# Induced attention and an ELU feed-forward: the opening stage rebuilt

## The chip, the core and the metric

The kernel runs on one core of one Trainium2 chip. The metric is the device time of one execution in microseconds; the kernel before has a median of 1762.04 us over 3 runs (1761.57 to 1762.32). Five engines have queues of their own: PE multiplies matrices, ACT evaluates functions, DVE and POOL work element by element, and SP issues the DMAs. An engine takes its instructions strictly in the order in which they stand in its queue.

## The reference

The input x has 4 batches of 12480 rows of 128 channels, in float32. A set of 32 learned rows ("inducing") first attends to all rows of a batch; then all rows attend to the 32 results. The output goes through a feed-forward layer of 2048 hidden units with an ELU between its two weights. Both weights arrive as float64.

```python
def mab(q, kv):
    s = scale * (q @ kv.transpose(0, 2, 1))
    s = s - s.max(-1, keepdims=True)
    a = np.exp(s); a /= a.sum(-1, keepdims=True) + 1e-09
    return a @ kv
h = mab(I, x)                  # 32 rows per batch
y = mab(x, h)                  # 12480 rows per batch
h1 = y @ w_in                  # 128 -> 2048
g = np.where(h1 > 0, h1, np.exp(np.minimum(h1, 0)) - 1)
return g @ w_out               # 2048 -> 128
```

## The kernel before, in words

A batch is cut into 25 blocks of 512 or 480 rows, gathered into 7 groups of up to 4 blocks (`GROUPS`). For every block the feed-forward runs over 8 units; a unit is a pair of 128-wide chunks of the 2048 hidden units. Within a unit, PE makes two chunks of the hidden layer in PSUM (line 560), ACT takes the exponential (568), DVE joins it with the hidden value (574), ACT rounds the result to a high part (583), DVE or POOL makes the low part (586, or 591 and 596), and PE multiplies both with the second weight, itself split into a high and a low part (618). After 8 units DVE transposes the block's output out of PSUM (625) and SP stores it. PE runs up to 5 units ahead with line 560. The feed-forward's output for the first unit is issued once three further units have gone into PE (`RAMP`).

While the feed-forward of one batch runs, the first attention of the next batch is worked on beside it, in steps that are placed by hand at fixed units (`first_half`, `attend`): x pieces come through two buffers (`xqp`, tag "xq"), DVE transposes them (241), PE makes scores (293), and so on. The first batch has nothing to hide behind. Its first attention stands alone in front of everything, in `first_batch`, together with the conversion of both weights from float64. This opening stage is what the change touches.

The opening, in program order, is this. SP loads half of the first weight, then x in 14 pieces (two into the buffers "xm", the others into buffers that the feed-forward uses later), then the other half. For each of the 7 groups PE transposes the pieces, ACT and DVE copy them out (270), PE makes the scores (293), ACT copies them (302), and DVE takes their maximum (306). The softmax over all 12480 rows is done in two phases (`PHASES`): groups 0 to 2 use the maximum of these three groups, groups 3 to 6 use the maximum over all, and the first phase's sum is then rescaled. `bias_of` makes the two maxima into biases (318, 324, 326). For each group ACT takes the exponential (347), DVE transposes it (360), and PE gathers the weighted sum of the rows (369), which DVE adds up (378, 380, 385). The sum is normed (411) and spread (417), giving hT4. The second attention for block 0 alone (`lone`) goes through lines 485, 493, 501, 502, 505, 512 to 515, 523, 526 and 528 and ends in the first "stack", the moving operand of line 560. `project_h` multiplies hT4 with the converted first weight (427), and `stack_h` copies the product by 12 DMAs (449) into `hw`, the stationary operand of line 560.

The weights are read as pairs of 32-bit words and converted with integer and float instructions, in slices of 256 columns (`WS`), eight slices for each weight. For each slice `take_apart` uses DVE for exponent (158) and mantissa bits (168), ACT for the sign (162), the low word (163) and two clamps of the exponent (164, 165), and POOL for the scale (172). `put_together` multiplies sign and scale on POOL (180), joins the words on DVE (181) and multiplies both on POOL (185). For the second weight ACT copies each 128-column chunk as the high part (212, 215), and POOL subtracts for the low part (216). All slices pass through two buffers ("w_part", in the pool `op`). Slices of the first weight are called for after each group's scores, one for each group. The second weight is loaded in four quarters, two into "xm" buffers and two into buffers of group 1's x pieces, all of which come free only once the gathers have read them; it is converted before the lone attention in program order.

The order in which instructions enter the queues of ACT, DVE, POOL and SP is not the program order. A planner simulates the kernel ahead of time: when an engine is free in that simulation, it takes the ready instruction that stands first in the program. On the chip this order is then fixed, whatever is ready. From the first feed-forward unit on PE's order is that of the program.

## Time and profile before

| | |
|---|---|
| median of 3 runs | 1762.04 us |
| profiled execution: time | 1761.6 us |
| profiled execution: span of all its instructions | 1759.5 us |
| PE busy in the span | 1659.5 us (94%) |
| DVE busy | 1551.8 us (88%) |
| ACT busy | 1425.0 us (81%) |
| POOL busy | 1331.7 us (76%) |

The span runs from the first to the last instruction that the profiler recorded; 2.1 us of the execution lie outside it. Busy time is what an engine's instructions took, without the issuing of DMAs. A busy PE is not necessarily at its peak, since its matmuls are pipelined. In rows of the trace, `out<-in` names the tiles that an instruction writes and reads, L12 is line 12 of the kernel before, and `[1.35 <-POOL ...]` says that the engine had stood idle for 1.35 us until that instruction of POOL released it.

### The profile page before, as it was taken

The page shows a single profiled execution, that of the slowest core. Times are in us where ns is not written, and L with a number is a line of the kernel's source. Part 1 is how long each engine was busy: PE and PEld are TensorE (multiplying, and loading weights), DVE is VectorE, ACT ScalarE, POOL GpSimd, SP SyncE. Part 2 cuts the span into 40 slices and gives each one's busy share as a digit, 9 for nine tenths or more (in the row PEclk, how much of TensorE's full clock was granted, in tenths as well). Part 3 has the DMA queues.
Part 4 walks back from the last instruction along what each step waited for, and adds up shares of the span by engine and source line. Part 5 has one row for each costly group of instructions (what it writes and reads, how often), then busy time and mean ns, then how long its engine had stood idle before and what let it go on. Part 6 is the DMA issues. An engine that isn't in the chain of part 4 may idle for free.

```text
span 1759.5 us, 22797 instructions
## 1 busy us (share of the span) xinstructions
PE 1659.5 (94%) x7480; PEld 1177.4 (67%) x7480; DVE 1551.8 (88%) x1635; ACT 1425.0 (81%) x1662; POOL 1331.7 (76%) x955
## 2 busy tenths in 40 slices
PE   6699999999999999999999999999999999989897
PEld 4356666677766766767676666667777776667676
DVE  6899989888999898889899998988899988888886
ACT  6778888788887887878787888878888888888786
POOL 3978877777787777777787787777778887766665
PEclk9599999999999999999999999999999999999999
DMA  7362323323234224232225232321221211111111
GB/s 248 65 98 48 66 56 51 73 44 78 53 54 72 60 49 77 41 53 71 66 42 88 44 65 60 52 49 41 58 53 18 45 22 32 25 23 34 21 17 17
DMA packets 384757, 98.12 MB, mean 56 GB/s; under 512 B 364864, under 2 KB 370784, under 8 KB 384384
## 3 DMA queue, kind: packets, MB, share of 16 engines
q1 hardware_dynamic: 384640, 96.68, 28.4%
q8 instruction: 59, 0.97, 0.2%
q14 instruction: 58, 0.48, 0.1%
HBM read 48.94 MB, written 25.56 MB: 42 GB/s over the span
## 4 chain that ended last, share of the span: by engine, by line
PE 73%; DVE 12%; ACT 5%; issue 3%; POOL 3%; DMA 3%; SPq 0%; DVEq 0%; ACTq 0%; POOLq 0%
PE po L618 51%; PE ph L560 18%; DVE gl L586 4%; ACT e L568 3%; DVE ph L574 2%; DVE e L574 2%; DVE xT L241 2%; ACT gh L583 1%; PE ps_hh L369 1%; PE ps_t L485 1%; PE ps_s L293 1%; POOL gl L596 1%; DMA w_raw<-in_moe_w_in_dram 1%; DMA xq<-in_x_dram 1%; DMA xm<-in_x_dram 1%
## 5 line engine op out<-in xcount | busy, mean ns | idle before, releaser
L568 ACT ACTIVATE e<-ph 128x1024 f32<-128x1024 f32 (+1 forms) x800 | 803.5, 1005 | 241.3 <-PE ph L560 237.9
L591 POOL TENSOR_SCALAR e<-e 128x1024 f32<-128x1024 f32 (+1 forms) x483 | 495.4, 1031 | 354.2 <-ACT gh L583 309.0
L596 POOL TENSOR_TENSOR gl<-e,gh 128x1024 fp32r<-128x1024 f32 (+1 forms) x300 | 704.4, 2348 | 19.8 <-PE po L618 0.9
L574 DVE SCALAR_TENSOR_TENSOR e<-ph,e 128x1024 f32<-128x1024 f32 (+1 forms) x483 | 571.5, 1187 | 75.1 <-ACT e L568 73.1
L560 PE MATMUL ph<-stk,hw 128*128 128x512 f32 (+1 forms) x1600 | 563.0, 433 | 60.7 <-DVE gl L586 43.7
L618 PE MATMUL po<-gh,wo_h 128*128 128x512 f32 (+1 forms) x1234 | 481.7, 390 | 10.5 <-ACT e L568 6.5
L618 PE MATMUL po<-gh,wo_l 128*128 128x512 f32 (+1 forms) x1234 | 478.9, 388 | 0.0
L560 PEld LDWEIGHTS ph<-stk,hw 128*128 128x128 f32 x1600 | 289.9, 189 | 247.1 <-issue 92.8
L574 DVE SCALAR_TENSOR_TENSOR ph<-ph,e 128x1024 f32<-128x1024 f32 (+1 forms) x317 | 378.3, 1196 | 47.7 <-ACT e L568 46.4
L586 DVE SCALAR_TENSOR_TENSOR gl<-ph,gh 128x1024 fp32r<-128x1024 f32 (+1 forms) x317 | 375.8, 1185 | 40.4 <-PE po L618 25.9
L618 PE MATMUL po<-gl,wo_h 128*128 128x512 f32 (+1 forms) x1234 | 379.1, 388 | 2.8 <-POOL gl L596 2.8
L618 PE MATMUL po<-e,wo_n 128*128 128x512 f32 (+1 forms) x732 | 336.3, 582 | 0.0
L583 ACT ACTIVATE gh<-e 128x1024 fp32r<-128x1024 f32 (+1 forms) x300 | 311.1, 1037 | 26.6 <-DVE e L574 21.9
L583 ACT ACTIVATE gh<-ph 128x1024 fp32r<-128x1024 f32 (+1 forms) x317 | 318.0, 1003 | 11.5 <-DVE ph L574 9.7
L618 PEld LDWEIGHTS po<-gh,wo_h 128*128 128x128 f32 x1234 | 232.4, 188 | 64.5 <-ACT s L302 5.6
L618 PEld LDWEIGHTS po<-gl,wo_h 128*128 128x128 f32 x1234 | 232.4, 189 | 49.1 <-POOL gl L596 3.9
L618 PEld LDWEIGHTS po<-gh,wo_l 128*128 128x128 f32 x1234 | 232.7, 189 | 46.3 <-issue 0.2
L618 PEld LDWEIGHTS po<-e,wo_n 128*128 128x128 f32 x732 | 138.1, 189 | 97.3 <-issue 84.0
L625 DVE STREAM_TRANSPOSE o<-po 128x512 f32<-128x512 f32 (+1 forms) x100 | 69.3, 693 | 11.8 <-PE po L618 11.8
L241 DVE STREAM_TRANSPOSE xT<-xq 128x1024 f32<-128x1024 f32 (+2 forms) x39 | 45.2, 1160 | 0.0
L369 PE MATMUL ps_hh<-xm,e 128*32 128x128 f32 (+2 forms) x872 | 33.3, 296 | 8.4 <-DVE bias L326 2.3
L369 PEld LDWEIGHTS ps_hh<-xm,e 128*32 128x32 f32 (+2 forms) x872 | 25.4, 117 | 20.1 <-issue 12.4
(94 smaller groups left out, 582.3 us busy)
## 6 DMA issues: line engine op xcount, KB each, us to landing
xm<-in_x_dram SPq DMA_DIRECT2D x32, 512.0 KB, 4.4
out_dram<-o SPq DMA_DIRECT2D x240, 64.0 KB, 2.0
xq<-in_x_dram SPq DMA_DIRECT2D x84, 128.0 KB, 3.6
out_dram<-o SPq DMA_DIRECT2D x160, 60.0 KB, 2.0
stk<-ahi SPq DMA_DIRECT2D x118, 64.0 KB, 2.0
xq<-in_x_dram SPq DMA_DIRECT2D x60, 120.0 KB, 3.4
stk<-ahi SPq DMA_DIRECT2D x80, 60.0 KB, 2.0
stk<-alo SPq DMA_DIRECT2D x59, 64.0 KB, 2.0
```

Of the source, the lines that this page charges most:

```text
L241: tc.keep_in_program_order(nc.vector.transpose(t, xq.rearrange("p u d -> p (u d)")))
L293: nc.tensor.matmul(ps[j * Q : (j + 1) * Q, :T], indT, block_xT(b, g0 + j), start=True, stop=True,)
L369: nc.tensor.matmul(ps[c * Q : (c + 1) * Q, :C], st["e", g][:np_, u * Q : (u + 1) * Q], st["xm", g, u - u % UP][:np_, u % UP, :], start=(u ...
L560: nc.tensor.matmul(ph[:, i], state[b]["hw"][:, f * P : (f + 1) * P], stacks[b, k], start=True, stop=True,)
L568: nc.scalar.activation(e, ph, AF.Exp, bias=-1.0)
L574: nc.vector.scalar_tensor_tensor(out=v["g"], in0=v["ph"], scalar=1.0, in1=v["e"], op0=ALU.max, op1=ALU.min)
L583: nc.scalar.activation(v["gh"], v["g"], AF.Copy, bias=-1.0)
L586: nc.vector.scalar_tensor_tensor(out=v["gl"], in0=v["g"], scalar=-1.0, in1=v["gh"].bitcast(F32), op0=ALU.add, op1=ALU.subtract,)
L591: nc.gpsimd.tensor_scalar(out=v["e"], in0=v["e"], scalar1=-1.0, scalar2=1.0, op0=ALU.add, op1=ALU.mult)
L596: nc.gpsimd.tensor_sub(v["gl"], v["e"], v["gh"].bitcast(F32))
L618: nc.tensor.matmul(po[:, :T], w, g, start=(cp == 0 and i == 0), stop=(cp == NCP - 1 and i == len(parts) - 1),)
L625: nc.vector.transpose(o.rearrange("p u d -> p (u d)"), po[:, :T])
```

## The change

The conversion becomes one function, `to_float32`, in slices of 512 columns (four for each weight). The sign is no longer looked up on ACT and multiplied in on POOL: DVE takes the top bit of the high word and puts it into the scale's bits, in one instruction with an AND and an OR. For each slice DVE now has four instructions (exponent, sign into scale, mantissa, joining of the words), ACT three and POOL one; the last product is on POOL for the first weight and on DVE for the second.

The order changes as well. Slices 0 and 1 of the first weight are called for behind the scores of groups 2 and 3; slices 2 and 3 behind all gathers. Both biases are made directly behind the scores, and for batch 0 the first softmax phase covers groups 0 to 4 in place of 0 to 2 (`FIRST_PHASE`). The other batches keep 0 to 2. All four loads of the second weight are issued right behind the first weight's second half, two into the "xq" buffers and two into "xm". The first step of the lone attention is followed by `project_h`, then come its other steps, `stack_h`, and last the conversion of the second weight, whose high and low parts are taken from the converted words in place.

```diff
--- before.py
+++ after.py
@@ -78,7 +78,7 @@
     SB = 6
     XB = 2
     STK = 6
-    PHASES = [range(0, 3), range(3, NG)]
+    FIRST_PHASE = {0: NG - 2}
     CALM = 8
 
     const = ctx.enter_context(tc.tile_pool(name="const", bufs=1))
@@ -138,84 +138,75 @@
-    WS = 256
+    WS = 512
     rebias = const.tile([P, 1], F32, name="rebias")
...
+    def to_float32(raw):
+
+        raw = raw.rearrange("p (f two) -> p f two", two=2)
+        lo, hi = raw[:, :, 0], raw[:, :, 1]
+        low = lo.bitcast(F32)
+        part = op.tile([P, WS], U32, tag="o", name="w_part")
+        scale = part.bitcast(F32)
+        nc.vector.tensor_scalar(
+            out=part, in0=hi, scalar1=20, scalar2=0x7FF,
+            op0=ALU.logical_shift_right, op1=ALU.bitwise_and,
+        )
+        nc.scalar.activation(low, lo, AF.Copy, scale=2.0**-52)
+        nc.scalar.activation(scale, part, AF.Relu, bias=rebias)
+        nc.scalar.activation(scale, scale, AF.Relu, bias=largest, scale=-1.0)
+        nc.gpsimd.tensor_scalar(
+            out=part, in0=scale, scalar1=-254.0, scalar2=-float(1 << 23),
+            op0=ALU.add, op1=ALU.mult,
+        )
+        nc.vector.scalar_tensor_tensor(
+            out=part, in0=hi, scalar=0x80000000, in1=part,
+            op0=ALU.bitwise_and, op1=ALU.bitwise_or,
+        )
+        nc.vector.tensor_scalar(
+            out=hi, in0=hi, scalar1=0xFFFFF, scalar2=0x100000,
+            op0=ALU.bitwise_and, op1=ALU.bitwise_or,
+        )
+        nc.vector.scalar_tensor_tensor(
+            out=low, in0=hi, scalar=2.0**-20, in1=low, op0=ALU.mult, op1=ALU.add
+        )
+        return low, scale
 
     def load_w_in(half):
         n = F // 2
         raw = hwp.tile([P, 2 * n], U32, tag="hw", name="w_raw")
         nc.sync.dma_start(raw, w_in[:, 2 * half * n : 2 * (half + 1) * n])
-        return [Weight(raw[:, i : i + 2 * WS]) for i in range(0, 2 * n, 2 * WS)]
-
-    def finish_w_in(s, w):
-        w.put_together(win_sb[:, s * WS : (s + 1) * WS])
+        return [raw[:, i : i + 2 * WS] for i in range(0, 2 * n, 2 * WS)]
+
+    def finish_w_in(s, raw):
+        low, scale = to_float32(raw)
+        nc.gpsimd.tensor_tensor(
+            out=win_sb[:, s * WS : (s + 1) * WS], in0=low, in1=scale, op=ALU.mult
+        )
 
     WC = WS // C
 
-    def load_w_out(quarter, pool, tag):
-        n = NFC // 4
-        raw = pool.tile([P, n, 2 * C], U32, tag=tag, name="w_raw")
-        rows = w_out[quarter * n * P : (quarter + 1) * n * P, :]
+    def load_w_out(part, pool, tag):
+        raw = pool.tile([P, WC, 2 * C], U32, tag=tag, name="w_raw")
+        rows = w_out[part * WS : (part + 1) * WS, :]
         dma = nc.sync.dma_start(raw, rows.rearrange("(c p) d -> p c d", p=P))
-        raw = raw.rearrange("p c d -> p (c d)")
-        return [Weight(raw[:, i : i + 2 * WS]) for i in range(0, 2 * n * C, 2 * WS)], dma
-
-    def finish_w_out(s, w):
-        t = small.tile([P, WC, C], F32, tag="wo", name=f"wo_{s}")
-        w.put_together(t.rearrange("p c d -> p (c d)"))
+        return raw.rearrange("p c d -> p (c d)"), dma
+
+    def finish_w_out(s, raw):
+        low, scale = to_float32(raw)
+        nc.vector.tensor_tensor(out=low, in0=low, in1=scale, op=ALU.mult)
         for i in range(WC):
             f = s * WC + i
+            t = low[:, i * C : (i + 1) * C]
             if f in WHERE_N:
-                nc.scalar.copy(wo_n[:, WHERE_N[f], :], t[:, i, :])
+                nc.scalar.copy(wo_n[:, WHERE_N[f], :], t)
             if f in WHERE_S:
                 n = WHERE_S[f]
-                nc.scalar.copy(wo_h[:, n, :], t[:, i, :])
-                nc.gpsimd.tensor_sub(
-                    wo_l[:, n, :], t[:, i, :], wo_h[:, n, :].bitcast(F32)
-                )
+                nc.scalar.copy(wo_h[:, n, :], t)
+                nc.gpsimd.tensor_sub(wo_l[:, n, :], t, wo_h[:, n, :].bitcast(F32))
 
 
     xT = {}
@@ -310,9 +301,14 @@
 
 
 
+
+    def phases(b):
+        n = FIRST_PHASE.get(b, 3)
+        return [range(n), range(n, NG)]
+
     def bias_of(b, i):
         st = state[b]
-        n = PHASES[i].stop
+        n = phases(b)[i].stop
         ps = bank(f"ps_pm_{b}_{i}")
         apart = small.tile([P, 4, NG], F32, tag="apart", name=f"apart_{b}_{i}")
         nc.vector.tensor_tensor(
...
@@ -679,63 +675,47 @@
         start(b)
         PIECES = [(g, v) for g in range(NG) for v in range(0, GROUPS[g][2] // Q, UP)]
         room = [(xmp, "xm")] * XB + [(gp, "e")] * EB + [(ghp, "gh")] * GHB + [(glp, "gl")] * GLB
-        NW = F // WS
-        win, wout = [], []
-        win += load_w_in(0)
+        win = load_w_in(0)
         for g, v in PIECES:
             load_xm(b, g, v, *room.pop(0))
         win += load_w_in(1)
-        wins = iter(range(NW))
-
-        def some_w_in():
-            s = next(wins, None)
-            if s is not None:
-                win[s].take_apart()
-                finish_w_in(s, win[s])
-
+        wout = [load_w_out(i, *[(xqp, "xq"), (xmp, "xm")][i // 2]) for i in range(F // WS)]
+        win = list(enumerate(win))
+        one, two = phases(b)
         for g in range(NG):
             transpose_first(b, g)
             scores(b, g)
             turn[0] += 1
-            some_w_in()
-            if g + 1 == PHASES[0].stop:
+            if g in (2, 3):
+                finish_w_in(*win.pop(0))
+            if g + 1 == one.stop:
                 bias_of(b, 0)
                 turn[0] += 1
-        for g in PHASES[0]:
+        bias_of(b, 1)
+        turn[0] += 1
+        for g in range(NG):
             weights_of(b, g)
             e_of(b, g)
             gather(b, g)
             turn[0] += 1
-            if g == 0:
-                bias_of(b, 1)
-                turn[0] += 1
-        for g in PHASES[1]:
-            weights_of(b, g)
         sum_es(b)
-        for g in PHASES[1]:
-            e_of(b, g)
-            gather(b, g)
-            turn[0] += 1
-            if g == NG - 3:
-                share_of(b)
-                turn[0] += 1
-        for s in range(NW):
-            some_w_in()
-        for quarter in range(4):
-            ws, last = load_w_out(quarter, *[(xmp, "xm"), (gp, "e")][quarter >= XB])
-            wout += ws
+        share_of(b)
+        turn[0] += 1
+        for s, raw in win:
+            finish_w_in(s, raw)
         norm_h(b)
         spread_h(b)
         turn[0] += 1
-        for s, w in enumerate(wout):
-            w.take_apart()
-            finish_w_out(s, w)
-        for _, step in attend(b, -1):
-            step()
+        lone_steps = attend(b, -1)
+        lone_steps[0][1]()
         turn[0] += 1
         project_h(b)
+        for _, step in lone_steps[1:]:
+            step()
         stack_h(b)
-        return last
+        for s, (raw, _) in enumerate(wout):
+            finish_w_out(s, raw)
+        return wout[-1][1]
 
     units = [(b, k, cp) for b in range(B) for k in range(NBLK) for cp in range(NCP)]
     last = first_batch(0)
```

## Rows read from the trace of the kernel before

**Rows 1.** Busy time of stretches: us, then each engine's busy us (instructions), granted clock, DMA.

```profile
53.10:68.50 15.40, 4.71 (x12) 1.21 (x12) 13.61 (x24) 9.12 (x26) 14.44 (x22) 0.50 0.40 112
68.50:99.70 31.20, 26.49 (x85) 15.81 (x86) 27.07 (x28) 24.76 (x33) 26.20 (x26) 0.81 0.32 55
99.70:123.30 23.60, 20.88 (x86) 14.28 (x86) 23.30 (x26) 18.32 (x22) 18.51 (x13) 1.00 0.56 84
30.00:99.70 69.70, 43.55 (x325) 26.18 (x320) 56.62 (x94) 51.00 (x104) 52.34 (x67) 0.71 0.45 95
400.00:500.00 100.00, 98.28 (x463) 73.49 (x462) 88.70 (x95) 82.74 (x95) 80.34 (x58) 1.00 0.27 60
...
40.00:70.00 30.00, 14.10 (x141) 8.33 (x144) 24.55 (x51) 20.57 (x57) 23.90 (x38) 0.50 0.56 111
```

**Rows 2.** Waits of PE from 55 to 75 us: total, times, longest us.

```profile
PE ph L560 <- DVE stk L528: 9.3, 1, 9.3
```

**Rows 3.** Timeline of DVE at the first output: start us, us.

```profile
99.70 0.69 DVE L625 STREAM_TRANSPOSE o<-po 128x512 f32<-128x512 f32 x1
```

**Rows 4.** Chain of waits from 26 to 84 us: start us, us, what.

```profile
44.34 0.41 POOL w_part L172
...
82.58 2.39 POOL gl L596
```

**Rows 5.** Groups of instructions, 30 to 80 us: count | busy us, mean ns | idle before.

```profile
L180 POOL TENSOR_TENSOR w_part<-w_part 128x256 f32<-128x256 f32 x12 | 8.9, 743 | 0.5
L216 POOL TENSOR_TENSOR wo_l<-wo,wo_h 128x128 fp32r<-128x128 f32 x14 | 7.2, 517 | 0.4
L181 DVE SCALAR_TENSOR_TENSOR w_raw<-w_raw 128x256 f32<-128x256 uint32 x12 | 7.1, 595 | 0.2
L185 POOL TENSOR_TENSOR wo<-w_raw,w_part 128x256 f32<-128x256 f32 x8 | 6.3, 783 | 0.2
...
L168 DVE TENSOR_SCALAR w_raw<-w_raw 128x256 uint32<-128x256 uint32 x12 | 5.6, 477 | 0.6 <-ACT w_part L162 0.2
...
L158 DVE TENSOR_SCALAR w_part<-w_raw 128x256 uint32<-128x256 uint32 x12 | 4.4, 373 | 3.8 <-POOL win_sb L185 2.7 <-POOL wo L185 0.6 <-DMA w_raw<-in_moe_w_in_dram 0.4
```

**Rows 6.** Timeline of DVE from 6 to 30 us, two conversion instructions.

```profile
7.25 0.42 DVE L181 SCALAR_TENSOR_TENSOR w_raw<-w_raw 128x256 f32<-128x256 uint32 x1
7.59 0.29 DVE L168 TENSOR_SCALAR w_raw<-w_raw 128x256 uint32<-128x256 uint32 x1
```

**Rows 7.** Timeline of the opening, all engines, 27 to 84 us.

```profile
27.49 1.42 DVE L360 STREAM_TRANSPOSE e<-s 128x512 f32<-128x512 f32 x2
...
30.16 0.46 ACT L162 ACTIVATE w_part<-w_raw 128x256 f32<-128x256 int32 x1 [0.40 <-DMA w_raw<-in_moe_w_in_dram]
...
32.12 0.55 ACT L302 COPY s<-ps_s 128x480 f32<-128x480 f32 x1
...
32.73 1.08 PE L369 MATMUL ps_hh<-xm,e 128*32 128x128 f32 x32 [1.89 <-ACT s L302]
...
36.51 10.97 SPq L236 DMA_DIRECT2D xq<-in_x_dram  x8
...
37.63 0.82 DVE L158 TENSOR_SCALAR w_part<-w_raw 128x256 uint32<-128x256 uint32 x1 [1.35 <-POOL win_sb L185]
...
53.09 0.86 DVE L411 TENSOR_SCALAR hn<-h,r 128x128 f32<-128x128 f32 x1
...
83.73 1.20 DVE L241 STREAM_TRANSPOSE xT<-xq 128x1024 f32<-128x1024 f32 x1
```

**Rows 8.** Groups of DVE's instructions, 53.1 to 68.5 us, the conversions.

```profile
L168 DVE TENSOR_SCALAR w_raw<-w_raw 128x256 uint32<-128x256 uint32 x4 | 2.6, 642 | 0.2
L181 DVE SCALAR_TENSOR_TENSOR w_raw<-w_raw 128x256 f32<-128x256 uint32 x4 | 2.0, 492 | 0.1
L158 DVE TENSOR_SCALAR w_part<-w_raw 128x256 uint32<-128x256 uint32 x4 | 1.4, 353 | 0.6 <-POOL wo L185 0.6
```

**Rows 9.** Groups of DVE's instructions, 68.5 to 99.7 us, one short instruction.

```profile
L513 DVE TENSOR_SCALAR sm<-sm 96x16 f32<-96x16 f32 x1 | 0.8, 787 | 0.0
```

More of the change, by code (lines that the diff above doesn't have):

```diff
@@ L145 @@
     nc.gpsimd.memset(largest, 254.0)
-    class Weight:
-        def __init__(self, raw):
-            self.raw = raw.rearrange("p (f two) -> p f two", two=2)
-        def take_apart(self):
-            lo, hi = self.raw[:, :, 0], self.raw[:, :, 1]
-            part = op.tile([P, 2, WS], U32, tag="o", name="w_part")
-            scale, sign = part[:, 0], part[:, 1]
-            nc.vector.tensor_scalar(
-                out=scale, in0=hi, scalar1=20, scalar2=0x7FF,
-                op0=ALU.logical_shift_right, op1=ALU.bitwise_and,
-            )
-            nc.scalar.activation(sign.bitcast(F32), hi.bitcast(I32), AF.Sign)
-            nc.scalar.activation(lo.bitcast(F32), lo, AF.Copy, scale=2.0**-52)
-            nc.scalar.activation(scale.bitcast(F32), scale, AF.Relu, bias=rebias)
-            nc.scalar.activation(
-                scale.bitcast(F32), scale.bitcast(F32), AF.Relu, bias=largest, scale=-1.0
-            )
-            nc.vector.tensor_scalar(
-                out=hi, in0=hi, scalar1=0xFFFFF, scalar2=0x100000,
-                op0=ALU.bitwise_and, op1=ALU.bitwise_or,
-            )
-            nc.gpsimd.tensor_scalar(
-                out=scale, in0=scale.bitcast(F32), scalar1=-254.0, scalar2=-float(1 << 23),
-                op0=ALU.add, op1=ALU.mult,
-            )
-            self.scale, self.low, self.top = scale.bitcast(F32), lo.bitcast(F32), hi
-            self.sign = sign.bitcast(F32)
-        def put_together(self, dst):
-            nc.gpsimd.tensor_tensor(out=self.sign, in0=self.sign, in1=self.scale, op=ALU.mult)
-            nc.vector.scalar_tensor_tensor(
-                out=self.low, in0=self.top, scalar=2.0**-20, in1=self.low,
-                op0=ALU.mult, op1=ALU.add,
-            )
-            nc.gpsimd.tensor_tensor(out=dst, in0=self.low, in1=self.sign, op=ALU.mult)
@@ L350, in weights_of @@
             AF.Exp,
-            bias=st["bias", int(g in PHASES[1])][:np_],
+            bias=st["bias", int(g in phases(b)[1])][:np_],
             scale=SCALE,
@@ L378, in gather @@
             nc.vector.tensor_copy(st["h"], ps[:, :C])
-        elif g == PHASES[1].start:
+        elif g == phases(b)[1].start:
             nc.vector.scalar_tensor_tensor(
@@ L388, in sum_es @@
         st = state[b]
-        n = PHASES[1].start
+        n = phases(b)[1].start
         es0 = small.tile([P, 1], F32, tag="es0", name=f"es0_{b}")
@@ L652, in first_half @@
             steps.append((at + 0.8, lambda g=g: scores(b, g)))
-            if g + 1 == PHASES[0].stop:
+            if g + 1 == phases(b)[0].stop:
                 first = at + 1.1
@@ L659, in first_half @@
             at += 0.4
-            gap = (till - at) / len(PHASES[i])
-            for g in PHASES[i]:
+            gap = (till - at) / len(phases(b)[i])
+            for g in phases(b)[i]:
                 steps.append((at, lambda g=g: weights_of(b, g)))
@@ L699, in first_batch @@
             turn[0] += 1
-            some_w_in()
-            if g + 1 == PHASES[0].stop:
+            if g in (2, 3):
+                finish_w_in(*win.pop(0))
+            if g + 1 == one.stop:
                 bias_of(b, 0)
                 turn[0] += 1
-        for g in PHASES[0]:
+        bias_of(b, 1)
+        turn[0] += 1
+        for g in range(NG):
             weights_of(b, g)
```

1 line of the change is left out of this document (removed).

## The prediction

> **What bounds the kernel now.** I read stretches of the span first, then the waits of PE and the chain of waits in the opening, and last the groups of instructions there. From 400 to 500 us PE is busy for 98.28 of 100 us, DVE for 88.70, ACT 82.74, POOL 80.34 [rows 1]. The long middle is PE's, and the change leaves its matmuls alone; what can be won lies in front of it. The first matmul of the feed-forward part starts at 68.5 us, after a wait of 9.3 us for one DVE instruction, the last of the first stack [rows 2]. The first output block leaves PSUM at 99.70 us [rows 3]. I use that time as the handle: right behind it DVE and PE are nearly full (23.30 and 20.88 of 23.60 us) [rows 1], so what moves it moves the end by as much.
>
> What sets 99.7 us? Between 44 and 83 us the chain of waits runs almost without a break through POOL: the weight conversion, then the feed-forward's own differences, which queue behind it [rows 4]. POOL is busy for 14.44 of the 15.40 us before the first feed-forward matmul and for 26.20 of the 31.20 us after it. The reader should look at DVE in the same rows: 13.61 of 15.40, 27.07 of 31.20 and 56.62 of the 69.70 us from 30.0 to 99.7 [rows 1]. It is next in line, with 13.1 us of holes. PE's granted clock is 0.50 (the 1.2 GHz level) from 40 to 70 us, in which PE was busy for 14.10 of 30 us [rows 1]; the change takes no matmul away there, so I leave that as it is.
>
> **The change, part by part.**
>
> *Sign by bits, and the second weight's last product on DVE: POOL.* From 30 to 80 us POOL spends 8.9 us on 12 sign products, 6.3 us on 8 last products of the second weight and 7.2 us on 14 differences [rows 5], beside scale steps and the first weight's last products. The sign products go and the 8 last products move to DVE: 15.2 us less. What stays is wider but not more. POOL is then no longer what ends last in the opening.
>
> *The same edits: DVE.* Early in the trace, undisturbed, DVE's conversion instructions took 0.42 us (two inputs) and 0.29 us (one input) at 256 columns [rows 6]. At 512 I take 0.70 and 0.55; the bounds are 0.42 and 0.84, and 0.29 and 0.58 (no more columns' cost, or all of it twice). An AND and an OR on two integer inputs in one instruction is not in the trace; I give it 0.70, the value of its nearest row, the two-input kind, with the same bounds. A 512-column slice of the first weight needs two of each kind, 2.5 us; one of the second weight a product more, 3.2 us. After 30 us that is 2 x 2.5 + 4 x 3.2 = 17.8 us bare. Before, 12 slices of 256 were 12 x (0.29 + 0.29 + 0.42) = 12.0 us bare and took 7.1 + 5.6 + 4.4 = 17.1 [rows 5]: 5.1 us of waiting inside 36 instructions while POOL was working. Now there are 28 instructions, and POOL has half the conversion work up to the feed-forward, but its full work there. I take 4.5 us (bounds 0 and 12, see the rivals): 22.3 us against 17.1, so DVE gains 5.2 us of work.
>
> The Trainium skill (GPSIMD Engine Reference, "Specifications") says that POOL shares its SBUF interfaces with VectorE and that the two contend when a DVE instruction has two SBUF inputs or runs in a two-port mode. The trace agrees: the two-input instruction rose from 0.42 to a mean of 0.595 us [rows 5, 6]. This speaks against a two-input product on DVE: by it, with the same rise of 42% on 16 two-input instructions of 0.70 us, the waiting is 4.7 us in place of 4.5, and what the one-input ones wait would come on top.
>
> *ACT.* The sign look-ups go, and two instructions of 256 become one of 512. ACT was not the bound; shorter waits are all I count.
>
> *First softmax phase over five groups.* Before, three softmax weights on ACT and two transposes on DVE (1.42 us) stood among the last x copies [rows 7]. They now come later, so the last scores come 1 to 2 us earlier. The first gather started at 32.73 us only, behind the score copies [rows 7], so a first bias that waits for five groups costs nothing up to about 31 us; past that it costs what it slips.
>
> *Second half of the first weight.* It landed at 30.1 us and its instructions stood in front of the score copies: ACT took them from 30.16 us, and the next score copy started at 32.12, 2 us late. Then the second bias waited on DVE behind an instruction that stalled 1.35 us for POOL and took 0.82, until 38.45 us [rows 7]. In the new order these slices come after the gathers. I take 4 us saved (at the worst wide instructions land in the same places, and it is 1), and with the part above the second bias stands near 33 us. The seven gathers then need 7 x (0.7 transpose + 0.3 sum) = 7 us of DVE beside 5 us of the first weight's slices: h is ready and scaled near 43 us, where it was 53.09 [rows 7].
>
> *Second weight behind the chain.* From 53.10 to 68.50 us four slices' DVE instructions (2.6 + 2.0 + 1.4 = 6.0 us) stood among those of the first stack [rows 8]. Behind the chain they can only fill holes, but each wide one can hold it for up to 0.7 us; I take 3 of the 6 us. The first feed-forward matmul starts at 43 + 15.4 - 3 = 55.4 us, 13 us earlier. The twelve stacking DMAs keep their count, and the product that feeds them still follows the first attention scores by one step.
>
> *What is late next.* The second weight is needed from the fourth feed-forward unit on, and by DVE's budget it is not done by 55 us. From 28.5 us, where DVE's backlog now begins, to the first output DVE has 56.62 + 5.2 + 1.4 (the two transposes, now behind 30 us) = 63.2 us to do. It was busy for 27.07 of 31.20 us (87%) and then for 23.30 of 23.60 (99%) [rows 1]; I take 96%, nearer to the second, as POOL's waits go: 65.8 us. The first output comes at 94.3 us, 5.4 us earlier. Of the 13 us that the chain wins, the ramp gives back about 8, because DVE now converts the second weight beside the first units.
>
> *Loads.* Two quarters of the second weight now go out on SP right behind the first weight, into the two buffers of the next batch's x pieces; the other two wait on SP for the first gather, and nothing behind them there is due before the stacking DMAs. The x pieces went out from 36.51 us on, 8 issues in 10.97 us [rows 7]; now they wait until two slices are converted, split and released. DVE first used one at 83.73 us [rows 7], 15 us behind the first feed-forward matmul, which is now about 70 us. So they must start by 59 us. I cost this at nothing; if they start later, see the rivals.
>
> **Sum.** The profiled execution had a span of 1759.5 us and a time of 1761.6, 0.4 us under the median of 1762.0. 1759.5 - 5.4 + 2.1 + 0.4 = 1756.6; I say 1756.5 us.
>
> **Rivals.**
>
> *DVE holds it up; slower.* Most of the second weight is left for the time after the first feed-forward matmul, where POOL runs instructions of 2.39 us [rows 4]. There a one-input DVE instruction on 16 columns took 0.787 us [rows 9], where 256 columns take 0.29; a wait of 0.6 us is thus in the trace. On all 20 instructions of the second weight it makes 12 us in place of 4.5, and DVE's sum 70.7 us. At 93% (half-way between the two shares above) that is 76 us, and the first output comes at 104.5, 4.8 us late: 1767 us. It decides from 25 to 27 us of conversion on DVE. Against it: in the stretch before the ramp, with POOL all but full, the mean wait was under half of that [rows 5].
>
> The contention that this rival needs is the one that the Trainium skill describes (GPSIMD Engine Reference, "Specifications").
>
> *The whole shift survives.* The order on DVE is made by a planner. If it fits the second weight into the chain's holes and DVE waits little (0 to 2 us), the sum is 59 us; at 97% that is 61, the first output comes near 89.5, and 10 to 12 us are kept: 1751 us. For it: DVE's 13.1 us of holes [rows 1]. Against it: DVE has more to do than before.
>
> *Nothing is left.* The next batch's x pieces are held until POOL has made the second slice's differences. If that is 64 us and not 59, DVE stands 5 us at its first transpose, with everything in order behind it: 1761.5 us. Or the planner puts conversions ahead of the chain again, so that "behind the chain" holds in the text of the program only; the chain wins 5 us, the ramp takes them back, and the time is the same.
>
> **Chances.** Forecast (1752.5 to 1758.5) 0.45, the whole shift 0.20, nothing left 0.20, slower 0.15. A difference of 0.2% (3.5 us) is about what a measurement of this kernel can tell from no change. Forecast and whole shift give faster 0.64 (a little of the forecast lies within 0.2%), same 0.21, slower 0.15. For 8 times in 10 I go from 1747 to 1764, past the whole shift and through half of the slower case; the bounds on waiting (0 to 12 us) alone would give 1751 to 1767.
>
> **What would show it.** Right: the second bias before 35 us; POOL busy well under 80% before the first feed-forward matmul, and that matmul near 55 us; DVE over 93% busy between it and the first output, with 512-wide conversions among the units; the first output near 94 us. Wrong: a first output before 91 us (DVE was not the bound), a DVE that stands for a DMA at the next batch's first transpose (loads), or 512-wide conversions of over 1.2 us each (contention). The prediction falls as a whole if the first feed-forward matmul comes after 62 us.

## The result and the profile after

The changed kernel takes 1768.33 us (median of 6 runs), the kernel before 1762.02 on the same chip: a ratio of 1.0036, 95% interval 1.0023 to 1.0049. It is slower by 6.3 us. I had predicted 1756.5 us, in a range from 1747 to 1764: the sign was wrong, and the time is outside the range.

The same four stretches as in [rows 1], of the changed kernel (us, busy us and instructions of PE, its weight loads, DVE, ACT, POOL; granted clock; DMA):

```profile
53.10:68.50 15.40, 8.03 (x74) 3.82 (x68) 10.92 (x24) 6.91 (x23) 9.76 (x17) 0.58 0.68 106
68.50:99.70 31.20, 20.24 (x55) 13.19 (x56) 24.51 (x28) 18.81 (x22) 15.77 (x12) 0.66 0.27 67
99.70:123.30 23.60, 22.27 (x91) 13.80 (x89) 21.30 (x24) 17.57 (x21) 18.28 (x13) 0.99 0.66 85
30.00:99.70 69.70, 39.52 (x295) 25.77 (x296) 50.50 (x85) 39.82 (x75) 32.20 (x36) 0.63 0.33 70
```

From 30.0 to 99.7 us POOL lost 20 of its 52 us and DVE 6 of its 57, and yet the kernel came later. All engines have more holes than before: the opening is now bound by who waits for whom. The conversions on DVE did not grow. Groups of DVE's instructions from 30 to 80 us (count, busy us, mean ns, idle before), to be set beside [rows 5]:

```profile
L165 DVE SCALAR_TENSOR_TENSOR w_part<-w_raw,w_part 128x512 uint32<-128x512 uint32 x6 | 4.2, 692 | 3.5 <-POOL w_part L161 3.5
L173 DVE SCALAR_TENSOR_TENSOR w_raw<-w_raw 128x512 f32<-128x512 uint32 x6 | 4.1, 680 | 0.0
L154 DVE TENSOR_SCALAR w_part<-w_raw 128x512 uint32<-128x512 uint32 x6 | 3.8, 667 | 0.3 <-POOL pm L273 0.3
L200 DVE TENSOR_TENSOR w_raw<-w_raw,w_part 128x512 f32<-128x512 f32 x4 | 2.6, 686 | 0.0
L169 DVE TENSOR_SCALAR w_raw<-w_raw 128x512 uint32<-128x512 uint32 x6 | 2.4, 419 | 0.0
```

They sum to 17.1 us, what the narrow ones took before. The time went into the chain. First PE's waits from 30 to 107 us (total, times, longest), then the timeline of the opening, single engines (start us, us). The last fence shows the seventh score copy and the second bias in the kernel before:

```profile
PE ps_hh L365 <- ACT s L293: 6.7, 1, 6.7
PE ph L556 <- DVE stk L524: 5.4, 1, 5.4
PE ps_ht L413 <- DVE hn L407: 4.2, 1, 4.2
PE ph L556 <- DMA stk<-alo: 3.9, 1, 3.9
```

```profile
30.96 0.17 DVE L322 TENSOR_REDUCE bias<-ps_pm 128x1 f32<-128x20 f32 x1
33.06 0.70 ACT L343 ACTIVATE s<-s,bias 128x512 f32<-128x512 f32 x1
...
35.88 0.68 ACT L343 ACTIVATE s<-s,bias 128x480 f32<-128x480 f32 x1
...
36.56 1.32 ACT L160 ACTIVATE w_part<-w_part,largest 128x512 f32<-128x512 f32 x2
37.78 0.65 ACT L158 ACTIVATE w_raw<-w_raw 128x512 f32<-128x512 uint32 x1
38.34 0.53 ACT L293 COPY s<-ps_s 64x480 f32<-64x480 f32 x1
38.92 1.93 PE L365 MATMUL ps_hh<-xm,e 128*32 128x128 f32 x32 [6.74 <-ACT s L293]
...
43.24 0.14 DVE L322 TENSOR_REDUCE bias<-ps_pm 128x1 f32<-128x28 f32 x1
...
61.65 0.28 DVE L407 TENSOR_SCALAR hn<-h,r 128x128 f32<-128x128 f32 x1
...
73.37 1.22 PE L556 MATMUL ph<-stk,hw 128*128 128x512 f32 x2 [5.44 <-DVE stk L524]
...
90.52 0.61 ACT L528 CAST ahi<-aT 96x512 fp32r<-96x512 f32 x1
...
106.69 0.71 DVE L621 STREAM_TRANSPOSE o<-po 128x512 f32<-128x512 f32 x1
```

```profile
33.37 0.54 ACT L302 COPY s<-ps_s 64x480 f32<-64x480 f32 x1
...
38.37 0.17 DVE L326 TENSOR_REDUCE bias<-ps_pm 128x1 f32<-128x28 f32 x1
```

The last score copy (64x480, the seventh group) ran at 33.37 us before and now stands behind five exponentials and, after them, three wide conversion instructions, at 38.34. The first gather waits 6.7 us for it, the second bias comes at 43.24 in place of 38.37, h is scaled at 61.65 (53.09 in [rows 7]), and the first output comes at 106.69, 6.99 us after the 99.70 of [rows 3]. From the second output on, every block is 6.6 to 7.0 us late, a rigid shift, up to the last seven, which are 7.5 to 8.0 us late. So the handle that I had chosen, the first output, holds in this execution, and nearly everything lies in front of it.

### The profile page after: what moved, and what is told of

Read it like the earlier page. It is cut to its first block, busy times and chain, and to the rows that moved or that the text cites. A ratio compares the mean times of both kernels' runs of the same rounds, so it can differ in the third digit from the quotient of the medians.

```text
span 1767.0 us, 22694 instructions
## 1 busy us (share of the span) xinstructions
PE 1664.1 (94%) x7480; PEld 1182.7 (67%) x7480; DVE 1549.8 (88%) x1623; ACT 1414.4 (80%) x1622; POOL 1311.6 (74%) x919
## 4 chain that ended last, share of the span: by engine, by line
PE 73%; DVE 14%; ACT 6%; issue 4%; POOL 2%; DMA 1%; SPq 0%; DVEq 0%; ACTq 0%; POOLq 0%
PE po L614 50%; PE ph L556 18%; DVE gl L582 4%; ACT e L564 3%; DVE e L570 3%; DVE ph L570 2%; DVE xT L232 2%; PE ps_s L284 1%; ACT gh L579 1%; PE ps_hh L365 1%; PE ps_t L481 1%; POOL gl L592 1%; PE ps_x L252 1%; POOL e L587 1%; DVE o L621 1%
```

## Experiments

Key times of all runs in us, before in the first row. They are read from one profiled execution of each kernel; the time is the median of all its executions, and the ratio goes by the kernel before as it was measured beside it. "ramp" is first output minus first feed-forward matmul.

| kernel | first gather | 2nd bias | h scaled | first ff | first output | ramp | time, median | ratio to before, 95% |
|---|---|---|---|---|---|---|---|---|
| before | 32.73 | 38.37 | 53.09 | 68.54 | 99.70 | 31.2 | 1762.0 | |
| after | 38.92 | 43.24 | 61.65 | 73.37 | 106.69 | 33.3 | 1768.3 | 1.0023 to 1.0049 |
| e1_three | 34.03 | 36.86 | 53.77 | 66.95 | 100.61 | 33.7 | 1764.8 | 1.0007 to 1.0024 |
| e2_five_only | 34.47 | 39.53 | 57.06 | 72.46 | 106.42 | 34.0 | 1768.5 | 1.0025 to 1.0053 |
| e3_behind | 37.41 | 39.94 | 57.02 | 70.14 | 100.23 | 30.1 | 1764.1 | 1.0007 to 1.0024 |
| e4_conv | 31.76 | 35.63 | 52.07 | 67.14 | 96.64 | 29.5 | 1757.9 | 0.9968 to 0.9986 |
| e5_pin | 34.10 | 36.92 | 53.82 | 67.14 | 98.34 | 31.2 | 1758.3 | 0.9970 to 0.9988 |
| e6_loads | 31.97 | 36.20 | 51.58 | 65.48 | 99.22 | 33.7 | 1759.5 | 0.9980 to 0.9998 |
| e8_after_stack | 31.85 | 35.71 | 48.03 | 58.93 | 106.49 | 47.6 | 1763.7 | 1.0007 to 1.0025 |
| e9_both | 31.50 | 34.45 | 46.46 | 58.07 | 105.36 | 47.3 | 1765.8 | 1.0014 to 1.0032 |
| e10_loads_pin | 31.79 | 36.01 | 51.38 | 65.30 | 94.68 | 29.4 | 1755.9 | 0.9958 to 0.9982 |
| e11_two | 31.83 | 35.69 | 51.63 | 62.64 | 104.26 | 41.6 | 1765.1 | 1.0011 to 1.0029 |
| e12_three | 32.34 | 36.20 | 53.21 | 66.22 | 102.40 | 36.2 | 1762.4 | 0.9993 to 1.0011 |
| e13_two_half | 31.73 | 34.68 | 46.43 | 63.15 | 105.49 | 42.3 | 1766.3 | 1.0013 to 1.0032 |
| e14_bias_back | 31.85 | 36.07 | 51.39 | 65.63 | 95.01 | 29.4 | 1755.9 | 0.9955 to 0.9980 |
| e15_five_back | 34.66 | 46.28 | 62.97 | 74.12 | 104.38 | 30.3 | 1764.5 | 1.0010 to 1.0028 |

**e1_three: the change without the five groups.**

```diff
-    FIRST_PHASE = {0: NG - 2}
+    FIRST_PHASE = {}
```

> The changed kernel with its first softmax phase put back to three groups; everything else of the change stays. Theory A (the five-group phase is the cause: the copy of the seventh group's scores on ACT, and with it the first gather on PE, come 6 us late): the first gather starts near 33 us instead of 38.9, the first feed-forward matmul at 64 to 68 us instead of 73.4, and the time is 1757 to 1762 us. Theory B (the 512-column conversion on DVE is the cause): the time stays at 1766 to 1770 us and the first output stays later than 104 us.

The first output moves from 106.69 back to 100.61 us: 6.1 of the 7.0 us are the five groups. The time falls by only 3.5 us (theory A had 1757 to 1762): in the profiled execution 3.0 us are lost again far behind, in the last batch (see the end).

**e2_five_only: the kernel before, with the five groups alone.** The diff's lines on phases(b), with nothing else; the share of the sums follows the last but one group of the second phase.

> The kernel before with the five-group first phase for the first batch alone (the sum of the exponentials is shared out one gather later, as the second phase has only two groups). Theory A: the seventh group's scores are copied after five exponentials, the first gather starts near 38 us instead of 32.7, and the time is 1766 to 1770 us. Theory B: no slower than 1763 us, since nothing of the conversion changes.

It costs 6.7 us at the first output and 6.5 in the time, as much as the whole change. The seventh copy is late again, but the first gather does not wait for it here: it came at 34.47 us and not near 38. ACT and DVE there:

```profile
31.16 0.17 DVE L330 TENSOR_REDUCE bias<-ps_pm 128x1 f32<-128x20 f32 x1
...
37.13 0.57 ACT L302 COPY s<-ps_s 64x480 f32<-64x480 f32 x1
```

**e3_behind: five groups, with the exponentials behind the seventh copy.** There are six score buffers (SB). The seventh copy needs the first one's, which is free only after the first exponential and its transpose, and these wait for the first bias.

```diff
-    SB = 6
+    SB = 7
...
-            weights_of(b, g)
+            with tc.issue_after(state[b]["copied"].ins):
+                weights_of(b, g)
```

> The changed kernel, five groups in the first phase, with a seventh score buffer and with ACT's exponentials of the first batch queued behind the copy of the seventh group's scores. Theory A in its narrow form (a late copy is the whole harm of five groups): the first gather starts at 34 to 36 us, the second bias before 37 us instead of 43.4, the time is 1759 to 1764 us. If the harm is that five groups bring the exponentials and gathers behind everything else anyway: the first gather stays at 37 us or later and the time at 1765 us or more. Theory B: 1766 to 1770 us.

```profile
34.21 0.54 ACT L293 COPY s<-ps_s 64x480 f32<-64x480 f32 x1
37.41 1.93 PE L365 MATMUL ps_hh<-xm,e 128*32 128x128 f32 x30 [5.31 <-DVE e L356]
```

With the copy at 34.21 us the second bias comes at 39.94 and not 43.24, and the first feed-forward matmul at 70.14: half of the 6.4 us by which five groups had moved it against e1 are won back. The rest this edit pays at least in part itself: the first gather now waits for the exponentials, and behind it on PE stands the second bias's own matmul, at 39.27 us. Neither expectation held whole: the gather (37.41), the bias (39.94) and the time (1764.1) came later than the narrow theory said, and the time earlier than its alternative. That the first output is even with e1's (100.23 and 100.61) is the ramp: 3.6 us shorter, by a cast that e5 is about.

**e4_conv: the kernel before, with the new conversion alone.** to_float32 and the slices of 512 columns as in the diff; order, phases and loads as before.

> The kernel before with the new conversion alone: 512-column slices, the sign by bits, the second weight's last product on DVE; phases, places and loads of the second weight as before. Theory A: POOL falls well under 14 us of 15.4 before the first feed-forward matmul, which comes at 62 to 67 us, and the time is 1755 to 1761 us. Theory B: DVE's added work shows, first output at 103 us or later, time 1765 to 1769 us.

1757.9 us, 3.1 us earlier at the first output: theory A held, and this part of the change is a gain. In the changed kernel it is paid away: at the first output -3.1 us by the conversion, +4.0 by the new order and loads (e1 against e4), +6.1 by the five groups.

**e5_pin: e1_three with one cast put ahead.** In the new order block 1's stack came late: its first step, the cast ahi, stood on ACT behind two more wide instructions, 17.2 us after the first feed-forward matmul (14.0 in e4).

```diff
+        cast = nc.scalar.copy(ahi, aT)
...
+        with behind_cast(n, 6):
             nc.scalar.activation(e, ph, AF.Exp, bias=-1.0)
...
+            with behind_cast(n, 5):
                 nc.scalar.activation(v["gh"], v["g"], AF.Copy, bias=-1.0)
```

> The changed kernel with three groups in the first phase (e1_three), and one thing more: on ACT, the rounding of block 6's unit and the exponential behind it are queued behind the cast (ahi) of the first group's stack, as they stand in the queue of the kernel with the conversion alone. Theory (the 4 us that the ramp loses in the new order are that cast, which stands behind two more wide ACT instructions): the cast starts about 14 us after the first feed-forward matmul and not 17.2, PE's wait for the stack's transfer falls from 3.9 to under 1 us, the first output comes near 97.2 us in place of 100.61, the time is near 1761.3. Rival (the ramp is slow by DVE or by the low clock, and the late stack only falls into it): the first output stays past 99.5 us and the time near 1764.5.

The cast now starts 15.3 us after the first feed-forward matmul. First output 98.34, 2.3 us earlier where the theory said 3.4; the wait for the stack fell less than expected, from the first line (e1) to the second (e5):

```profile
PE ph L556 <- DMA stk<-alo: 3.9, 1, 3.9
```

```profile
PE ph L565 <- DMA stk<-alo: 2.4, 1, 2.4
```

The time fell by 6.5 us; the loss in the last batch did not occur in this profiled execution.

**e6_loads: e4_conv with the early loads alone.**

```diff
-            raw, last = load_w_out(quarter, *[(xmp, "xm"), (gp, "e")][quarter >= XB])
+            raw, last = load_w_out(quarter, *[(xqp, "xq"), (xmp, "xm")][quarter // 2])
```

The loop with this line also moves up, right behind the first weight's loads.

> The kernel with the 512-column conversion alone, old order and three groups (e4_conv), with the loads of the changed kernel: the second weight's four parts go out on SP right behind the first weight, two into the buffers of the next batch's x pieces, two into the first gathers' pieces. Theory (the early data is what lets the planner put the second weight's conversions among the gathers; the place in the program's text does nothing): h scaled near 54 us in place of 52.07, the cast of the first group's stack later, the first output between 99 and 101 us in place of 96.64, time near 1762. Rival (as I predicted: the loads cost nothing, it is the place of the first weight's second half and of the projection in the text that costs): first output at 96.6, time 1758.

The theory had the first output (99.22) but neither the way to it nor the time (1759.5, not 1762). h comes at 51.58 and the first feed-forward matmul at 65.48, 1.7 us before e4's, so the gather chain is not slowed. But the ramp is 4.2 us longer: on SP two x pieces go out ahead of block 1's stack, on ACT the cast is late again (16.5 us after the first feed-forward matmul), and PE waits for that stack.

```profile
81.77 0.94 SPq L227 DMA_DIRECT2D xq<-in_x_dram  x2
82.80 3.20 SPq L529 DMA_DIRECT2D stk<-ahi  x5
86.10 1.17 SPq L529 DMA_DIRECT2D stk<-alo  x2
```

```profile
PE ph L551 <- DMA hw<-hw_h: 8.2, 1, 8.2
PE ph L551 <- DMA stk<-alo: 4.9, 1, 4.9
```

**e10_loads_pin: e6_loads and the pin of e5_pin.**

> e6_loads (conversion alone with the early loads of the second weight) and the cast of the first group's stack ahead of the next two wide instructions on ACT, as in e5_pin. e6_loads had its first feed-forward matmul 1.7 us before the kernel with the conversion alone and its first output 2.6 us after it; PE waited 4.9 us for the stack's transfer. Theory (that wait is the late cast and nothing else): the wait falls to 0.5 to 2.5 us, the first output comes near 96.5 us (99.22 without), time near 1757. Rival (the transfer is late because loads of x pieces stand ahead of it on SP): the wait stays over 4 us and the first output over 98.5.

```profile
94.68 0.70 DVE L627 STREAM_TRANSPOSE o<-po 128x512 f32<-128x512 f32 x1
```

The pin brings 4.5 us at the first output (theory: 2.7); the wait for the stack is 2.9 us. With the pin the two x pieces also went behind the stack on SP, so how much of the 4.5 us is the cast and how much the x pieces is not separated. This version beats both kernels: 1755.9 us, 6.3 under before.

**e14_bias_back: e5_pin with the second bias behind the first gather again.** e5 and e10 still differed by 3.7 us. bank() hands out two PSUM banks in turn; the change had moved bias_of(b, 1) ahead of the gathers.

```diff
-        bias_of(b, 1)
-        turn[0] += 1
         for g in range(NG):
...
+            if g == 0:
+                bias_of(b, 1)
+                turn[0] += 1
```

> e5_pin (the changed kernel with three groups in the first phase and the first group's cast ahead on ACT) with one thing put back: the second bias stands behind the first gather in the text, as in the kernel before. e5_pin and e10_loads_pin differ by 3.7 us at the first output (98.34 and 94.68) though both have the new conversion, the early loads and the pinned cast. Theory (the two PSUM banks are taken in turn, so a bias that takes its turn ahead of the gathers puts the first gather into the bank of the seventh group's scores in place of the sixth's; the place of the weight slices and of the projection in the text does nothing): first gather at 31.8 us in place of 34.10, first output near 94.7, time near 1756. Rival (the slices' place in the text costs the 3.7 us): first output stays near 98, time near 1758.3.

The first gather in e5, then that and the first output in e14:

```profile
34.10 1.28 PE L366 MATMUL ps_hh<-xm,e 128*32 128x128 f32 x32 [2.95 <-ACT s L294]
```

```profile
31.85 1.08 PE L366 MATMUL ps_hh<-xm,e 128*32 128x128 f32 x32 [0.58 <-ACT s L294]
...
95.01 0.69 DVE L632 STREAM_TRANSPOSE o<-po 128x512 f32<-128x512 f32 x1
```

The theory held: the first gather is back at 31.85, the time at 1755.9. With its turn ahead, the bias had moved the first gather into the bank of the seventh group's scores, so it waited for that copy (34.10 in e5, 38.92 in the changed kernel). The rest of the new text, the slices' place and the projection ahead of the exponentials, is in this kernel too, and it ends 0.3 us from e10_loads_pin, which has none of it: it neither costs nor brings anything.

**e15_five_back: e14_bias_back with the five groups.**

> The changed kernel, five groups and all, with the cast pinned and the second bias behind the first gather: what five groups cost with neither of the two other losses. Theory (the five groups cost by themselves, because the seventh score copy waits for one of six score buffers, and with it the second bias): first output 6 to 7 us after that of e14_bias_back, near 101, time near 1762. Rival (five groups cost only through the first gather that stands behind the seventh copy): first output within 2 us of e14_bias_back, near 96, time near 1757.

```profile
38.34 0.55 ACT L294 COPY s<-ps_s 64x480 f32<-64x480 f32 x1
...
46.28 0.17 DVE L323 TENSOR_REDUCE bias<-ps_pm 128x1 f32<-128x28 f32 x1
```

The first gather is early (34.66), but the seventh copy is again at 38.34, the second bias at 46.28 and the first output at 104.38, 9.4 us after e14. So the five groups cost by themselves, more than I expected; the bank is a second path to the same copy. The late copy is not all of it: the second bias starts 2.6 us after the copy's start in e14, 4.9 in the changed kernel and 7.9 here, where conversions on DVE and a gather on PE stand between them.

**e8_after_stack and e9_both: the order that I had predicted, forced.** Both from e4_conv; the second also holds the first weight's second half behind the second bias on DVE and the last score copy on ACT.

```diff
+        with tc.issue_after(state[b]["stacked"].ins):
+            for s, w in enumerate(wout):
+                finish_w_out(s, w)
```

> The conversion alone (e4_conv) with the lone block's steps and the projection ahead of the second weight in the text, and the second weight's DVE instructions queued behind the last DVE instruction of the first stack: behind the chain in the queue and not only in the text. Theory (my step on what is late next holds): h scaled by 50.5 us (52.07 with the conversion alone), first feed-forward matmul near 62 (67.14), but the 13 us of conversion now stand among the first units, DVE is over 85% busy there and the first output wins 0 to 2 us only: 94.6 to 96.6, time 1756 to 1758. Rival 1 (DVE has room in the ramp): all 5 us stay, first output below 93, time near 1753. Rival 2 (the units wait for the second weight on PE): first output after 98, time over 1759.

> As e8_after_stack, and the first weight's second half queued behind the second bias on DVE and behind the last score copy on ACT: the order that I had predicted for the change, forced. Theory (my steps for the second half and for the chain hold where the order is really taken): second bias near 33.5 us (35.63 with the conversion alone), h scaled near 48, first feed-forward matmul near 60 (the projection still waits for the first weight's last slices), first output 1 us before that of e8_after_stack, time near 1755.5. Rival (the projection waits for the first weight, so nothing of the earlier bias is left): h earlier by 2 us, first feed-forward matmul and time as e8_after_stack.

The chain comes near what I said: first feed-forward matmul at 58.93 and 58.07 us, my sum gave 55.4. But the ramp grows to 47.6 and 47.3 us. PE's waits from 55 to 125 us in e8_after_stack, and the stretch of its ramp:

```profile
PE po L609 <- ACT wo_h L208: 14.8, 2, 9.6
```

```profile
58.90:106.50 47.60, 29.07 (x84) 17.31 (x84) 41.37 (x46) 31.49 (x50) 32.97 (x33) 0.70 0.32 66
```

DVE is busy for 41.4 of 47.6 us, 87%; PE stands for the second weight. Rival 2 of e8 was right. And here DVE's conversions are slow: the second weight's 20 take 17.8 us, where at the durations that they have alone in the changed kernel they would take 11.6. Two of them in e8:

```profile
69.05 2.02 DVE L173 SCALAR_TENSOR_TENSOR w_raw<-w_raw 128x512 f32<-128x512 uint32 x1
70.99 1.26 DVE L169 TENSOR_SCALAR w_raw<-w_raw 128x512 uint32<-128x512 uint32 x1
```

In e9 the earlier second bias brings 1.1 us at the first output; its median is nevertheless 2.1 us above e8's, while of the profiled executions e9's has the shorter span (1764.4 and 1765.6 us; e8's is the slowest of its eleven, which start at 1763.3). I leave that open.

**e11_two, e12_three and e13_two_half: only the last two parts, or only the last one, behind the stack**, and e11 with e9's hold.

```diff
+        for s, w in enumerate(wout[:2]):
+            finish_w_out(s, w)
+        with tc.issue_after(state[b]["stacked"].ins):
+            for s, w in enumerate(wout[2:], 2):
+                finish_w_out(s, w)
```

> e8_after_stack with only the last two of the second weight's four parts queued behind the first stack on DVE; the first two stay where the scheduler puts them. In e8_after_stack the first feed-forward matmul came at 58.93 us, but PE then waited 14.8 us for the converted second weight. Theory (the second weight is needed unit by unit, so the half that the first four units need is due early and the rest is not): first feed-forward matmul near 63 us, a wait for the second weight under 4 us, first output near 94.5 us, time near 1756, 2 us under the kernel with the conversion alone. Rival (whatever goes behind the stack comes back as a wait of PE): first output at 97 us or later, time 1758 or more.

> As e11_two with only the last of the four parts behind the first stack. Theory: first feed-forward matmul near 65 us, no wait for the second weight over 1 us, first output near 95.5, time near 1757. Rival (the order of the rest moves as well and the stack's cast comes late, as in e6_loads): PE waits over 3 us for the stack's transfer and the first output is past 97.

> e11_two with the first weight's second half behind the second bias on DVE and behind the last score copy on ACT, as in e9_both, where this brought 1.1 us at the first output. Theory: the same 1 us again, first output 1 us before e11_two, time 1 us less. Rival (it moves the second weight back too, and PE waits for that): no gain, or a first output after that of e11_two.

My theories missed the first output and the time in all three; the rivals held. No wait for the second weight of a microsecond is left, but each part behind the stack lengthens the ramp: 36.2 us with one part, 41.6 with two, 47.6 with four, against 29.5 with none; the wait for block 1's stack is 3.7, 4.7 and 6.8 us in e12, e11 and e13. Conversion work is cheap in the chain's holes and dear in the ramp.

## Why the prediction was wrong, point by point

- **First softmax phase over five groups: the step that failed.** I wrote that a first bias that waits for five groups "costs nothing up to about 31 us". It came at 30.96, inside that bound, and cost 6.1 us (e1; 6.7 alone, e2). I looked at what the first gather waits for and not at what the first bias holds up: the seventh group's copy needs one of six buffers, so it cannot run before an exponential, and on ACT it ended up behind all five. e3 wins half back with the copy ahead of them, and e15 shows 9.4 us where neither the bank nor the cast adds to it.
- **Second half of the first weight: failed.** I expected the second bias near 33 us; it came at 43.24, and even in e9, where the order was forced, at 34.45. From there to the scaled h I booked 10 us, though my own terms, 7 us for the gathers and 5 for the slices, add up to 12, and e9 took 12.0. The text's place of these slices moved nothing: in the changed kernel their instructions still surround the seventh copy. I also passed over the moved second bias in the diff, whose turn put the first gather into another bank (3.3 us at the first output, e5 against e14).
- **Second weight behind the chain: it held in the text only.** I had this as a part of the rival "Nothing is left". All of its conversions ran before the first feed-forward matmul, at 73.37 us, not at 55.4. Most stood among the gathers: from the second bias to h it took 18.4 us (16.4 in e4, 12.3 in e8, where they stand behind the stack). From h to the first feed-forward matmul it took 11.7 us, close to my 12.4, but not because conversions had gone behind it: luck. "The prediction falls as a whole if the first feed-forward matmul comes after 62 us": it did.
- **What is late next.** The direction was right, the size was not: I let the ramp give back 8 of 13 us; forced, it gave back about 18 (ramp 47.6 against 29.5) and made the kernel slower. DVE's busy share there was 87%, not 96: PE waits for the high part on ACT, the end of a chain over three engines, which a budget of DVE alone doesn't show.
- **Loads: not nothing.** They brought the chain 1.7 us and cost the ramp 4.2 (e6 against e4); both went through the order of queues, on ACT and SP, not through late x pieces, which DVE never waited for.
- **DVE and POOL: mis-sized, in my favour.** POOL's relief was real. DVE's conversion took 17.1 us where I had 22.3: the AND and OR took 0.69 us (I took 0.70), the one-input ones 0.42 at best (0.55), and waiting was small: 25 of the 28 instructions took 0.41 to 0.69 us, as alone, and three L154 took 1.57, 0.68 and 0.50 in place of 0.42, 1.5 us more in all, where I took 4.5. The rival "DVE holds it up; slower" named the right sign by a mechanism that did not occur in the changed kernel. It did occur where the order that I had forecast was forced: in e8 the 20 conversions of the second weight took 6.2 us longer than alone, and the rival had 12. So my 4.5 us came out too high with the conversions in front of the ramp, where POOL rested beside most of them, and would have been too low in the order that I forecast: luck. I had also read [rows 5] and [rows 6] in part only: a one-input instruction (L168) rose there too, from 0.29 to 0.477 us. The Trainium skill (GPSIMD Engine Reference, "Specifications") names DVE instructions with two SBUF inputs or in a two-port mode as those that contend with POOL. In the changed kernel the two-input conversions stayed at 0.66 to 0.69 us; in e8 the long ones were of both kinds, and no run here shows whether the one-input ones ran in such a mode.
- **The handle was right** within an execution: the shift at the second output (6.66 us) is still there in the last batch (6.58), up to its last seven blocks. Between executions it is rough: e8's first output was 6.8 us late in an execution of 1767.4 us, while its median is 1763.7. e14 has every part of the change but the five groups and the moved bias, and a pinned cast besides; that its time, 1755.9 us, lies beside my 1756.5 is by other terms (first feed-forward matmul 65.63, ramp 29.4), not by mine: luck.

What stays open: why the planner put the exponentials and the cast where it did; whether a seventh buffer alone would move the copy, as e3 changed buffer and order at once; and which of the three engines sets the ramp's length in e11 to e13, where no single wait explains 12 us.

## What to carry to other kernels

When a step is made to wait for more input, list what its output frees as well as what reads it: with fewer buffers than groups, a later bias holds the copy that the next bias needs. Before predicting from a moved line, see whether the queues change: buffers, PSUM turns and load times moved this kernel's queues, and the place of the conversions in the text moved none that mattered. Try the parts of a change singly; here one part gained 4 us and another lost 6.

## What the runs showed of the hardware

A wait in the opening can be paid twice. The first gather of 32 small matmuls took 1.93 us in the changed kernel, after a wait of 6.7 us of which the first row shows the last 2.9, and 1.08 in e14, after a wait of 0.58; the granted clock was 0.50 (1.2 GHz) and 1.00 (2.4 GHz). The length of the wait alone does not set it: after 2.79 us it took 1.94 in e1 (granted clock 0.50), after 2.95 us it took 1.28 in e5 (0.79).

```profile
36.00:38.90 2.90, 0.00 (x0) 0.00 (x0) 0.85 (x2) 2.87 (x6) 1.39 (x2) 0.50 0.00 0
38.90:40.90 2.00, 1.93 (x32) 1.36 (x32) 1.62 (x4) 0.00 (x0) 0.34 (x1) 0.50 0.00 0
```

```profile
31.80:33.00 1.20, 1.08 (x32) 0.81 (x32) 0.66 (x2) 1.20 (x3) 0.00 (x0) 1.00 0.00 0
```

A conversion on DVE can take three times as long beside POOL. In e8's ramp six conversions took 1.26 to 2.02 us, where such instructions take 0.42 or 0.69 alone. Each of the six began while a POOL instruction ran and ended 0.3 to 0.6 us after that one, as if it had waited for it; but one that also began beside POOL, at 77.02 us, took 0.68. These are POOL's instructions beside the two rows of e8 above:

```profile
67.85 2.66 POOL L587 TENSOR_TENSOR gl<-e,gh 128x1024 fp32r<-128x1024 f32 x1
70.48 1.49 POOL L582 TENSOR_SCALAR e<-e 128x1024 f32<-128x1024 f32 x1
```

In the profiled executions of e1 and e3 the rigid shift grew by 3.0 and 2.9 us at one block of the last batch: one wait of PE for DVE of 3.2 us, and a granted clock of 0.90 in that stretch (shown for e1) where the other kernels have 1.00. In e5 the longest such wait was 1.4 us and the shift stayed. What tips it I did not find. That the order of the instructions decides it is not shown: eleven executions of e1, the same program, lie between 1762.4 and 1766.2 us.

```profile
1573.00:1590.00 17.00, 13.80 (x48) 9.70 (x47) 16.07 (x16) 12.18 (x15) 10.47 (x8) 0.90 0.14 23
```
